# Output weights and gated products moved to another start address in larger tiles, in a three-stage attention and MoE kernel

## The chip, the cores and the metric

One core of one Trainium2 chip. The metric is the device time of one execution in microseconds (us), first instruction to last with what lies around them; less is better.

## What is computed

A linear attention with exponential features, then two gated feed-forward layers one after the other, all in float32:

```python
def _attn_ref(q, k, v, w_phi):            # 4 batches, 8 heads, 576 tokens, 64 per head
    ...
    num = einsum('bhsf,bhfd->bhsd', q_p, kv)
    den = einsum('bhsf,bhf->bhs', q_p, z)[..., None] + 1e-06
    return num / den
def _moe_ref(x, w_gate, w_val, w_out):    # x 2304 x 512, w_gate and w_val 512 x 1536, w_out 1536 x 512
    g = x @ w_gate
    return (silu(g) * (x @ w_val)) @ w_out
def _moe2_ref(x, w_gate, w_val, w_out):   # the same with sigmoid(g) in place of silu(g)
    ...
```

The output is `_moe2_ref(_moe_ref(attention))`, 2304 x 512.

## The kernel before

The first 150 us are attention. From there to the end TensorE runs the two layers, in four passes (`hh` 0 to 3; 0 and 1 are layer one, 2 and 3 layer two, each pass with half of the 1536 inner columns). A pass goes over five token blocks, four of 512 tokens and one of 256, and in each over three pairs of inner column groups (`p` 0 to 2). One `(hh, j, p)` is called a unit here; a layer has 24 units of a full block and 6 of the short block.

Every float32 operand is split into a high and a low part, and each product is made of three matmuls (high by high, high by low, low by high). A unit of a full block has

- seven products of a Strassen-like scheme (`product`, L1024), each twice, 84 matmuls of 256 columns. Their stationary operands are 128 x 128 pieces of the tiles `w0h`, `w0l` (and `w1`, `w2` for the other pairs), their moving operands are pieces of `xh`, `xl`;
- 24 matmuls of the output product of the unit before it (`accumulate`), put between the products in groups of 12, 9 and 3 by the tuple `ORDER`. In layer one (L1099) the output weights `o0h`, `o0l` are stationary and the gated products `uh`, `ul` move; in layer two (L1101) `uh`, `ul` are stationary and `o` moves, 512 columns each.

A unit of the short block has four products, 48 matmuls, and 12 accumulations of 512 columns (24 of 256 in layer one).

Between them ScalarE and VectorE bring products out of PSUM (`keep`, `add`), apply the gate, multiply (`gated`) and split the result into `uh`, `ul` (`gated_split`, `plan_halves`, L579 and L573). Output weights come to `o..l` by a DMA on SP's queue (`load_out`, L632) and are split in place by the same two engines; in the first slots they are made in place of being loaded (`split_home`). All DMAs of the kernel are issued on SP's queue; the order of all work is written out by hand in `TIMES`, one due time for each call.

Where operands lie in a partition follows from the tile sizes. The first 16384 bytes are scratch for DMA descriptors, then come four constants of 32 bytes each, so the pools `w0` and `w1` begin 128 bytes past a multiple of 256. All tiles of `w0`, `w1` and `w2` have sizes that are multiples of 512 bytes, and each matmul operand in them begins at a multiple of 512 bytes in its tile. So every `w` and `o` operand begins at 128 modulo 256 (`w2` on the right side too). The pool `stage` adds 192 bytes beyond multiples of 256 (two small tiles of 96), so every `x` and `u` operand begins at 64 modulo 256.

Of the kernel before, what the change touches and what calls it, by code (L numbers as in the profile page):

```python
# [11 lines left out]
R32 = mybir.dt.float32r  # L12
# [8 lines left out]
P = 128  # L21
# [3 lines left out]
DM = H * D  # L25
# [36 lines left out]
NQ = 256  # L62
# [14 lines left out]
ORDER = ((1, 2, "a", "b", 5, "c", "d", 4),  # L77
         (1, 5, "a", "b", 6, 3, 7, 2, "c", "d0", 4, "d1"))
ORDER_LAST = (1, 5, "a", 6, 3, "b", 7, 2, "c", 4, "d")


def as_float(bits):
# [349 lines left out]
class Plan:  # L432
# [10 lines left out]
    def at(self, t, fn, *args):  # L443
        if self.given:
            t = next(self.given[fn.__name__])
        self.events.append((t, len(self.events), fn, args))
# [7 lines left out]
def body(ctx: ExitStack, tc: tile.TileContext, qT, kT, v, w_phi2, wpk, out):  # L454
    nc = tc.nc
# [9 lines left out]
    pools = {w: ctx.enter_context(tc.tile_pool(name=w, bufs=1)) for w in ("w0", "w1")}  # L465
# [37 lines left out]
    def piece(name, dt=F32):  # L503
        return stage.tile([P, 1024], dt, tag="raw", name=name, bufs=RB)

    def scratch(name, dt=F32):
        return stage.tile([P, 768], dt, tag="tmp", name=name, bufs=TB)
# [62 lines left out]
    wts = {}  # L570

    def low(hi, lo, src):
        nc.vector.tensor_tensor(out=lo, in0=src, in1=hi, op=ALU.subtract)  # L573

    def plan_halves(t, views):

        def high():
            hi, _, src = views()
            nc.scalar.copy(hi, src)  # L579

        def rest():
            low(*views())

        at(t, high)
        at(t + 0.6, rest)

    def plan_slot(t, hh, p, gap=3.0, out=14.0):

        l, q = hh // 2, (hh % 2) * NPAIR + p
        a, s = {}, {}

        def home(i):
            w = i // 2
            if w not in a:
                a[w] = piece("a").rearrange("p (c q n) -> p c q n", c=2, q=4) if w < 2 else \
                    piece("a").rearrange("p (c n) -> p c n", c=2)
            return a[w][:, i % 2] if w == 2 else a[w][:, i % 2].rearrange("p q n -> p (q n)")  # L600

        def load(w):
            a[w] = piece("a").rearrange("p (c q n) -> p c q n", c=2, q=4)
            assert stored >= {("w", l, q, 2 * w), ("w", l, q, 2 * w + 1)}
            nc.sync.dma_start(out=a[w], in_=wf[l][q][:, w])

        begins = not isinstance(t, float)

        def sums(w):

            s[w] = scratch("s").rearrange("p (c q n) -> p c q n", c=2, q=3)
            a21, a11, a12, a22 = (a[w][:, :, k] for k in range(4))
            s1, s2, s4 = (s[w][:, :, k] for k in range(3))
            tt = (nc.gpsimd if begins else nc.vector).tensor_tensor
            tt(out=s1, in0=a21, in1=a22, op=ALU.add)
            tt(out=a21, in0=a11, in1=a21, op=ALU.subtract)
            tt(out=s2, in0=s1, in1=a11, op=ALU.subtract)
            tt(out=s4, in0=a12, in1=s2, op=ALU.subtract)

        def split(w, m):  # L620
            if (hh, p) not in wts:
                wts[hh, p] = [pools[f"w{p}"].tile([P, 2, 2, 7, P], R32, tag=f"w{p}{x}",
                                                  name=f"w{p}{x}{hh}") for x in "hl"]
            d, src = ((slice(0, 4), a), (slice(4, 7), s))[m]
            return *(x[:, w, :, d] for x in wts[hh, p]), src[w]

        def load_out():
            pool = pools[f"w{p}"]
            wts[hh, p, "o"] = [pool.tile([P, 2, DM], R32, tag=f"o{p}{x}", name=f"o{p}{x}{hh}")
                               for x in "hl"]  # L630
            assert stored >= {("w", l, q, 4), ("w", l, q, 5)}
            nc.sync.dma_start(out=wts[hh, p, "o"][1].bitcast(F32), in_=wfo[l][q])  # L632

        def split_out():
            hi, lo = wts[hh, p, "o"]
            return hi, lo, lo.bitcast(F32)

        def split_home():
            if (hh, p, "o") not in wts:
                wts[hh, p, "o"] = [pools[f"w{p}"].tile([P, 2, DM], R32, tag=f"o{p}{x}",  # L640
                                                       name=f"o{p}{x}{hh}") for x in "hl"]
            return *wts[hh, p, "o"], a[2]

        if not isinstance(t, float):
            for i, u in enumerate(t):
                e = plan_round(u, l, q, i, home)
                if i < 4 and i % 2:
                    at(e + 0.8, sums, i // 2)
                    for m in range(2):
                        plan_halves(e + 2.4 + 1.5 * m, partial(split, i // 2, m))  # L650
                elif i == 5:
                    plan_halves(e + 1.0, split_home)
            return

        for w in range(2):
            at(t + 2 * gap * w, load, w)
            at(t + 4.0 + 2 * gap * w, sums, w)
            for m in range(2):
                plan_halves(t + 6.0 + gap * (2 * w + m), partial(split, w, m))
        at(t + out, load_out)  # L660
        plan_halves(t + out + 4.0, split_out)

# [403 lines left out]
        v, o = places(r, j, 1, d)  # L1066
        nc.vector.tensor_tensor(out=o, in0=v, in1=places(r, j, 0, d)[1], op=ALU.mult)  # L1067

    def gated_split(r, j, f):
        n = BLOCKS[j][1]  # L1070
        v = r["c", f][:, 1].rearrange("p t n -> p (t n)")[:, :n]
        if ("u", f) not in r:
            r["u", f] = [pools["u"].tile([P, 2 * NQ], R32, tag=f"u{x}{f}", name=f"u{x}{f}")[:, :n]
                         for x in "hl"]
        return *r["u", f], v

    def part_of_group(m, s):
# [77 lines left out]
    def plan_out(t, r, hh, j, p, group):  # L1155

        n = BLOCKS[j][1]
        f, h = divmod("abcd".index(group[0]), 2)
        s = group[1:]
        at(t, accumulate, r, hh, j, p, f, h, s)  # L1160
        t += (3 if s else 6) * n / NQ * PT
        if s != "0" and p == NPAIR - 1 and f == 1 and not goes_on(hh + 1, j):
            if hh < 2:
                tiles = range(2) if h == 1 else ()
            else:
                tiles = (h,) if n == 2 * NQ else range(h)
            for i, k in enumerate(tiles):
                if hh % 2 == 1 and not goes_on(hh, j):
                    at(t - 8.0, out_load, hh, j, k)
                at(t + 0.1 + 1.2 * i, out_sum, hh, j, k)  # L1170
                at(t + OS + 1.5 * i, out_store, hh, j, k)
        return t

    def plan_unit(t, r, hh, j, p, last):


        full = BLOCKS[j][1] == 2 * NQ
        done = set()
        for k in ORDER_LAST if (hh, j, p) == (3, len(BLOCKS) - 1, NPAIR - 1) else ORDER[full]:
            if isinstance(k, str):  # L1180
                if last:
                    t = plan_out(t, *last, k)
                continue
            done.add(k)
            for w in range(2):
                at(t, product, r, hh, j, p, w, k)
                t += 6 * PT
            e = t + 0.1
            if full and k in (1, 5, 6):
                at(e, keep, r, k)  # L1190
            if full and k in (2, 3, 7):
                at(e, add, r, {2: 0, 3: 1, 7: 3}[k])
                e += 0.7
            for d in ([3] if full and k == 7 else [2] if k == 4 else
                      [0] if k in (2, 3) and done >= ({2, 3} if full else {2}) else []):
                at(e, gate, r, hh, j, d)
                at(e + 0.6, gated, r, j, d)
                if d != 3:
                    plan_halves(e + 1.2, partial(gated_split, r, j, d // 2))
        return t  # L1200

    def pool(name, side="left"):
# [23 lines left out]
    for hh in range(4):  # L1226
        begin.append(t)
        for i, j in enumerate(ROUTE[hh]):
            if hh % 2 == 1 and i < 2:
                xs[hh, j] = None  # L1230
            elif last:
                xprep.append((t, hh, j))
            for p in range(NPAIR):
                r = {}
                t = plan_unit(t, r, hh, j, p, last)
                free[hh, p] = t
                last = r, hh, j, p
# [13 lines left out]
    n = 6 * NPAIR  # L1251
    when = [R0A + (T0 - R0Z - R0A) * m / n for m in range(n)]
    for p in range(NPAIR - 1):
        plan_slot(when[6 * p:6 * p + 6], 0, p)
    for m in range(n - 6, n):
        plan_round(when[m], 0, NPAIR - 1, m % 6)
    plan_x_block(T0 - X00, 0, 0, XG)
    plan_slot(T0 - 3.0, 0, 2)
    for t, hh, j in xprep:
        plan_x_block(t - XL, hh, j, XG)  # L1260
    for hh in range(1, 4):
        plan_rounds(hh, begin[hh - 1] + RA, begin[hh] - RZ)
        for p in range(NPAIR):
            plan_slot(free[hh - 1, p] + SO, hh, p, SG)
# [43 lines left out]
```

## Time and profile before

| | us |
|---|---|
| median of 3 runs | 996.61 (989.23 to 996.86) |
| the profiled execution | 996.62 |
| its span, first instruction to last | 994.5 |
| TensorE matmul busy | 980.9 |
| VectorE busy | 692.4 |
| ScalarE busy | 527.2 |

All that the trace says is of the profiled execution. A matmul's busy time overlaps with that of the next, since matmuls are pipelined; what one costs in a stream is the time from its start to the start of the next, or a piece of the chain of work divided by its matmuls.

### The profile page before, as it was taken

Reading aid. Unit: us, or ns where it says so; the run is one execution under the profiler, and the core shown is the slowest. Engines: PE = TensorE matmul, PEld = TensorE weight load, DVE = VectorE, ACT = ScalarE, POOL = GpSimd, SP = SyncE. Lnnn points to the kernel's source line nnn. Section 1 sums busy time; section 2 is a strip of 40 time slices with the busy share of each in tenths; the row PEclk is TensorE's granted clock in tenths of the full one; section 3 lists DMA queues with packets and bytes.
Section 4 is the critical chain, followed back from the end, with each engine's and each line's share of the span. In section 5 each row is a group of like instructions: output and inputs, shape, how many; then the busy total and the mean of one; then the engine's idle time right before and its main releaser. Section 6 shows DMA issues by size and latency. Waiting matters only on the chain.

```text
span 994.5 us, 20911 instructions
## 1 busy us (share of the span) xinstructions
PE 980.9 (99%) x8632; PEld 891.5 (90%) x8632; DVE 692.4 (70%) x1220; ACT 527.2 (53%) x977; POOL 38.8 (4%) x40
## 2 busy tenths in 40 slices
PE   7999999999999999999999999999999999999998
PEld 6777778999999999999999999999999999999997
DVE  6999888938757795368787897486677834555343
ACT  5988977535545564264454574455546534334321
POOL 1433210000000000000000000000000000000000
PEclk9999999999999999999999999999999999999999
DMA  7566876436535532066554442446416002132011
GB/s 239 167 216 211 262 240 197 149 126 182 196 118 153 183 96 83 1 198 213 155 174 134 167 156 77 141 141 197 144 70 191 23 21 86 64 128 86 1 44 42
DMA packets 67551, 136.00 MB, mean 137 GB/s; under 512 B 9408, under 2 KB 35712, under 8 KB 67456
## 3 DMA queue, kind: packets, MB, share of 16 engines
q1 hardware_dynamic: 67456, 134.68, 42.4%
q8 instruction: 67, 1.10, 0.4%
q14 instruction: 28, 0.23, 0.1%
HBM read 94.66 MB, written 39.99 MB: 135 GB/s over the span
## 4 chain that ended last, share of the span: by engine, by line
PE 95%; DVE 3%; DMA 1%; ACT 0%; issue 0%; SPq 0%; DVEq 0%; ACTq 0%
PE a L1024 30%; PE b L1024 23%; PE c L1101 8%; PE c L1099 8%; PE d L1099 8%; PE d L1101 6%; PE d L787 5%; PE c L724 3%; PE w L688 3%; DVE sub L697 1%; DVE m L695 1%; PE w L751 1%; DMA xT<-nd 1%; DMA x<-kT 0%; ACT eq L771 0%
## 5 line engine op out<-in xcount | busy, mean ns | idle before, releaser
L1050 DVE TENSOR_TENSOR c<-b,c 128x512 f32<-128x512 f32 x96 | 66.0, 687 | 118.9 <-PE b L1024 109.9
L1062 ACT ACTIVATE c<-c 128x256 f32<-128x256 f32 x96 | 50.3, 525 | 147.0 <-DVE c L1050 147.0
L1044 ACT COPY c<-a 128x512 f32<-128x512 f32 x96 | 56.4, 587 | 111.9 <-PE a L1024 109.3
L573 DVE TENSOR_TENSOR ul<-c,uh 128x512 fp32r<-128x512 f32 (+1 forms) x120 | 75.8, 635 | 33.3 <-ACT uh L579 32.5
L579 ACT CAST uh<-c 128x512 fp32r<-128x512 f32 (+1 forms) x120 | 69.3, 580 | 41.6 <-DVE c L1067 33.3
L1024 PE MATMUL a<-xh,w0h 128*128 128x256 f32 x288 | 80.7, 280 | 0.0
L1024 PE MATMUL a<-xh,w1h 128*128 128x256 f32 x288 | 80.5, 280 | 0.0
L1024 PE MATMUL a<-xh,w2h 128*128 128x256 f32 x288 | 80.5, 279 | 0.0
L1024 PE MATMUL a<-xl,w0h 128*128 128x256 f32 x288 | 80.3, 279 | 0.0
L1024 PE MATMUL a<-xl,w2h 128*128 128x256 f32 x288 | 80.3, 279 | 0.0
L1024 PE MATMUL a<-xl,w1h 128*128 128x256 f32 x288 | 80.3, 279 | 0.0
L1024 PE MATMUL a<-xh,w0l 128*128 128x256 f32 x288 | 80.2, 279 | 0.0
L1024 PE MATMUL a<-xh,w2l 128*128 128x256 f32 x288 | 80.2, 279 | 0.0
L1024 PE MATMUL a<-xh,w1l 128*128 128x256 f32 x288 | 80.2, 278 | 0.0
L1067 DVE TENSOR_TENSOR c<-c 128x256 f32<-128x256 f32 (+1 forms) x96 | 52.9, 555 | 29.4 <-ACT c L1062 29.4
L1024 PE MATMUL b<-xh,w0h 128*128 128x256 f32 x224 | 62.5, 279 | 0.0
L1024 PE MATMUL b<-xh,w0l 128*128 128x256 f32 x224 | 62.4, 279 | 0.0
L1024 PE MATMUL b<-xh,w2l 128*128 128x256 f32 x224 | 62.4, 279 | 0.0
L1024 PE MATMUL b<-xh,w1l 128*128 128x256 f32 x224 | 62.4, 279 | 0.0
L1024 PE MATMUL b<-xl,w0h 128*128 128x256 f32 x224 | 62.4, 279 | 0.0
L1024 PE MATMUL b<-xh,w1h 128*128 128x256 f32 x224 | 62.4, 278 | 0.0
L1024 PE MATMUL b<-xl,w1h 128*128 128x256 f32 x224 | 62.4, 278 | 0.0
(183 smaller groups left out, 3028.5 us busy)
## 6 DMA issues: line engine op xcount, KB each, us to landing
raw<-wpk SPq DMA_DIRECT2D x72, 512.0 KB, 5.0
wf<-wcv SPq DMA_DIRECT2D x40, 256.0 KB, 2.8
a<-wf SPq DMA_DIRECT2D x20, 512.0 KB, 5.3
b<-xo SPq DMA_DIRECT2D x16, 512.0 KB, 6.1
part<-o SPq DMA_DIRECT2D x13, 512.0 KB, 6.2
o<-part SPq DMA_DIRECT2D x13, 512.0 KB, 4.7
wfo<-wcv SPq DMA_DIRECT2D x20, 256.0 KB, 4.9
v<-v SPq DMA_DIRECT2D x18, 264.0 KB, 7.3
```

Source lines behind the costliest of these rows:

```text
L573: nc.vector.tensor_tensor(out=lo, in0=src, in1=hi, op=ALU.subtract)
L579: nc.scalar.copy(hi, src)
L688: nc.tensor.matmul(r["ps"][:, i, n, c], r["x"][d, c, n * P:(n + 1) * P], w2[d], start=True, stop=True)
L724: nc.tensor.matmul(kv[qd, b][h // 2][u * 64:(u + 1) * 64, c * P:c * P + VW], e[r0:r1, h % 2, n, h // 2, s, u], r["v"][r0:r1, n, h], start= ...
L787: nc.tensor.matmul(pn[i * w:(i + 1) * w, :m], f, e[:, h, c, :m], start=(c == 0), stop=(c == 1))
L1024: nc.tensor.matmul(o, f[:, c], x[:, c], start=k == first and w == 0 and c == 0 and m == 0, stop=c == 1 and m == 2, skip_group_check=True)
L1044: nc.scalar.copy(part_of(r, d), parts(r, src))
L1050: nc.vector.tensor_tensor(out=c, in0=parts(r, "zy x"[d]), in1=c, op=ALU.add)
L1062: nc.scalar.activation(o, g, AF.Silu if hh < 2 else AF.Sigmoid)
L1067: nc.vector.tensor_tensor(out=o, in0=v, in1=places(r, j, 0, d)[1], op=ALU.mult)
L1099: nc.tensor.matmul(ps[:, :n], a[:, k], x, start=st, stop=sp)
L1101: nc.tensor.matmul(ps, x[:, k], a, start=st, stop=sp)
```

## The change

Each tile of output weights `o` and of gated products `u` becomes 128 elements (512 bytes) longer. The `o` operand begins 48 elements (192 bytes) into its tile, in both layers; the `u` operand stays at the start of its tile. 128 + 192 = 320, so `o` operands now begin at 64 modulo 256, as `x` and `u` do; `w` operands stay at 128. The DMA scratch shrinks from 16384 to 1024 bytes, by a multiple of 256, which makes room for the larger tiles. No instruction is added, removed or moved.

```diff
+U_AT = (0, 0)
+O_AT = (48, 48)
...
+        def out_tiles():
+            o = O_AT[l]
+            wts[hh, p, "o"] = [pools[f"w{p}"].tile([P, 2 * DM + P], R32, tag=f"o{p}{x}",
+                                                   name=f"o{p}{x}{hh}")[:, o:o + 2 * DM]
+                               .rearrange("p (c n) -> p c n", c=2) for x in "hl"]
+
         def load_out():
-            pool = pools[f"w{p}"]
-            wts[hh, p, "o"] = [pool.tile([P, 2, DM], R32, tag=f"o{p}{x}", name=f"o{p}{x}{hh}")
-                               for x in "hl"]
+            out_tiles()
...
         def split_home():
             if (hh, p, "o") not in wts:
-                wts[hh, p, "o"] = [pools[f"w{p}"].tile([P, 2, DM], R32, tag=f"o{p}{x}",
-                                                       name=f"o{p}{x}{hh}") for x in "hl"]
+                out_tiles()
             return *wts[hh, p, "o"], a[2]
...
-    def gated_split(r, j, f):
+    def gated_split(r, hh, j, f):
         n = BLOCKS[j][1]
         v = r["c", f][:, 1].rearrange("p t n -> p (t n)")[:, :n]
         if ("u", f) not in r:
-            r["u", f] = [pools["u"].tile([P, 2 * NQ], R32, tag=f"u{x}{f}", name=f"u{x}{f}")[:, :n]
-                         for x in "hl"]
+            o = U_AT[hh // 2]
+            r["u", f] = [pools["u"].tile([P, 2 * NQ + P], R32, tag=f"u{x}{f}", name=f"u{x}{f}")
+                         [:, o:o + n] for x in "hl"]
         return *r["u", f], v
...
-    nc = bacc.Bacc("TRN2", target_bir_lowering=False, num_devices=1)
+    nc = bacc.Bacc("TRN2", target_bir_lowering=False, num_devices=1, dynamic_dma_scratch_size=1024)
```

## Rows read from the trace of the kernel before

**Rows 1.** Page, busy time (share) x instructions of each engine.

```profile
PE 980.9 (99%) x8632; PEld 891.5 (90%) x8632; DVE 692.4 (70%) x1220; ACT 527.2 (53%) x977; POOL 38.8 (4%) x40
```

**Rows 2.** Page, chain that ended last: share of the span by engine.

```profile
PE 95%; DVE 3%; DMA 1%; ACT 0%; issue 0%; SPq 0%; DVEq 0%; ACTq 0%
```

**Rows 3.** Waits in total: who waited for whom, us, times, longest.

```profile
DVE c L1050 <- PE b L1024: 109.9, 34, 6.9
```

**Rows 4.** Stretches: length; PE, PEld, DVE, ACT, POOL busy; granted clock; DMA; GB/s.

```profile
200.00:300.00 100.00, 100.00 (x736) 94.69 (x735) 63.96 (x128) 48.54 (x101) 0.00 (x0) 1.00 0.50 159
...
700.00:800.00 100.00, 100.00 (x715) 93.38 (x714) 73.86 (x132) 55.12 (x96) 0.00 (x0) 1.00 0.30 98
```

**Rows 5.** Chain in order of time (start, us, what), layer one, full block.

```profile
212.90 1.42 PE a L1024 x12
214.31 1.41 PE b L1024 x12
215.73 1.39 PE c L1099 x6
...
226.27 1.37 PE a L1024 x12
...
228.33 1.42 PE a L1024 x12
```

**Rows 6.** Chain in order of time, layer two, full block.

```profile
618.53 1.39 PE a L1024 x12
619.91 1.36 PE b L1024 x12
621.27 1.37 PE c L1101 x6
622.65 1.37 PE d L1101 x6
...
633.62 1.39 PE a L1024 x12
```

**Rows 7.** Chain in order of time, layer one, short block.

```profile
259.23 1.41 PE a L1024 x12
...
267.71 1.41 PE a L1024 x12
```

**Rows 8.** Chain in order of time, layer two, short block.

```profile
678.91 1.39 PE a L1024 x12
...
687.15 1.39 PE a L1024 x12
```

**Rows 9.** Chain in order of time, before and after layer one's first accumulation.

```profile
156.04 1.36 PE a L1024 x12
...
172.17 1.42 PE a L1024 x12
```

**Rows 10.** Chain in order of time, where layer two's accumulations begin.

```profile
591.04 1.40 PE c L1101 x6
...
593.84 1.38 PE a L1024 x12
595.22 1.36 PE b L1024 x12
```

**Rows 11.** Instructions on PE in order of time, layer two: start, duration, line, names.

```profile
614.12 0.28 PE L1024 MATMUL b<-xh,w2l 128*128 128x256 f32 x1
614.23 0.39 PE L1101 MATMUL c<-o1h,uh 128*128 128x512 f32 x1
...
616.06 0.39 PE L1101 MATMUL d<-o1l,uh 128*128 128x512 f32 x1
616.29 0.28 PE L1024 MATMUL a<-xh,w2h 128*128 128x256 f32 x1
```

**Rows 12.** Instructions on tile o0l from 400 to 600 us: duration min/median/max, starts.

```profile
L579 ACT CAST o0h<-o0l x1: 1043/1043/1043, 562.8 to 562.8; 128x1024 fp32r<-128x1024 f32 x1
L573 DVE TENSOR_TENSOR o0l<-o0l,o0h x1: 1216/1216/1216, 574.0 to 574.0; 128x1024 fp32r<-128x1024 f32 x1
```

More of the change, by code (lines that the diff above doesn't have):

```diff
@@ L1198, in plan_unit @@
                 if d != 3:
-                    plan_halves(e + 1.2, partial(gated_split, r, j, d // 2))
+                    plan_halves(e + 1.2, partial(gated_split, r, hh, j, d // 2))
         return t
```

## The prediction

> **What bounds the kernel now.** I read the page first. TensorE is busy 99% of the span [rows 1] and holds 95% of the chain that ended last [rows 2]. The others wait for it: the largest wait of VectorE is 109.9 us for products [rows 3]. In the two layers no slice of TensorE is idle and the granted clock is 1.00, the higher level of 2.4 GHz, in both [rows 4]. So the only thing that a change of addresses can move is the pace of back-to-back matmuls, and that pace passes to the end almost whole.
>
> Next I read the chain in order of time, whose pieces give that pace. The same 12 products, same shapes, operands at the same places modulo 256 bytes, take 1.41 or 1.42 us in one place of layer one and 1.37 in another, 12 matmuls later in the same unit [rows 5]; in layer two they take 1.39 right after accumulations and 1.36 otherwise [rows 6]. That is 117.5 ns for a matmul at the one pace, called the 1.41 pace here, and 113.3 at the other, the 1.36 pace. A row of products mostly keeps the pace at which it begins. What sets it is the accumulations before it. Before layer one's first accumulation products run at 1.36; after it at 1.42 [rows 9]. Where layer two's accumulations begin, the first six still take 1.40, and the products after them 1.38 and then 1.36 [rows 10]; from there on each row of products is at the 1.36 pace after its first matmuls. So the two layers' accumulations leave TensorE at different paces, and they differ in one thing that an address can carry: what moves while what is loaded. In layer one `u` moves (64 modulo 256) while pieces of `o` are loaded (128); in layer two `o` moves (128) while `u` is loaded (64).
>
> The reader can see the whole price in two subtractions. A full unit, from its first product to that of the next, takes 228.33 - 212.90 = 15.43 us in layer one [rows 5] and 633.62 - 618.53 = 15.09 in layer two [rows 6], for the same 84 products and 24 accumulations of 512 columns. A short unit takes 8.48 [rows 7] and 8.24 [rows 8], for the same columns.
>
> **The change part by part.** *The scratch* shrinks by a multiple of 256, so it moves no operand modulo 256; all DMAs are on SP's queue and POOL issues none. Nothing is taken or added: 0.
>
> *The larger `u` tiles* keep `u` at 64: 0.
>
> *Writing and loading `o` at the new place.* A load, a cast and a subtraction for each of 12 slots. They are early: `o0h`'s cast runs at 562.8 for 1.04 us and the subtraction for `o0l` at 574.0 for 1.22 [rows 12], and layer two's first accumulation with them comes at 591.04 [rows 10]. Some 16 us cover them. Were both twice as long, nothing would move; without that cover they would cost the 2.3 us that they last, 27 us over 12 slots. I take 0.
>
> *Reading `o` at the new place* is all that is left. Now in both layers moving and loaded operand of an accumulation both begin at 64. At the edges: during the last product before a group, `x` (64) moves while `o` or `u` (64) is loaded; during the last accumulation of a group an operand at 64 moves while `w` (128) is loaded, in both layers.
>
> Two of these pairings stand in the trace at one matmul each. Equal places occur in layer two: the last product before a group has `x` moving and `u` loaded, both at 64, and the next matmul starts 0.11 us later, no stall [rows 11]. The last accumulation has `o` moving and `w` loaded, both at 128; the next starts 0.23 us later, and six of its kind take 1.37 [rows 6], so 0.228 each: no stall either [rows 11]. And after that matmul products settle at the 1.36 pace every time. Nothing shows a whole group at equal places; I bound it by the nearest rows: six accumulations between 1.36 (the columns of twelve products at the 1.36 pace) and 1.40 [rows 10]. I take 1.37, since the equal pairings that do occur cost no more than that.
>
> For the pace that the products get, the bounds are layer one's and layer two's. I take layer two's for both layers, because its groups end in an equal pairing and always leave the 1.36 pace. It is a choice: after the change a group's last matmul pairs 64 with 128, as layer one's does now.
>
> Sum: layer one at layer two's unit times. 24 full units x 0.34 us = 8.2; 6 short units x 0.24 = 1.4; together 9.6 us. The profiled execution took 996.62 (span 994.5 and 2.1 around it), within 0.01 of the median: 996.6 - 9.6 = 987.0.
>
> A rule speaks against any gain. The Trainium skill, page "SBUF — State Buffer", section "Who interferes with whom", gives TensorE two independent read ports, one for the moving operand and one for weight loads, and says that it never waits on anyone. By that rule start addresses are nothing and the sum is 0; the trace has 1.41 and 1.36 for equal products [rows 5, 6], which such ports alone don't explain, though it doesn't show that addresses are the cause either. The page "TensorE: Matmul & The Clock Gate", section "Back-to-back issue gap", gives a gap of N / 2.4 + 2.5 ns, 109.2 at 256 columns and 215.8 at 512; an estimate by it is 14.4 us for a full unit, which no row here reaches.
>
> **The rivals.**
>
> *Layer two falls to layer one's pace.* After the change both layers have the same places, so one pace may hold for both, and it may be 1.41: the group's last matmul (64 moving, 128 loaded) is the pairing that layer one has throughout. For it: in layer one that pairing leaves the 1.41 pace after groups of 12 and of 3 (1.42 and 1.41) [rows 5]. Against it: after the group of 9 it leaves the other (1.37) [rows 5]. It decides if rows of products in layer two start at 1.41 and stay. Then layer two takes layer one's unit times, 24 x 0.34 + 6 x 0.24 = 9.6 more: 1006.2. If the one row of 1.36 in each full unit goes as well, 0.05 x 48 = 2.4 more: 1008.6.
>
> *The paces alternate, or nothing changes.* In layer one the pace after a group alternates with the number of matmuls in it: 1.41 after 12, 1.36 after 9, 1.41 after 3. If the alternation stood the other way, six of the seven dozens of products in a unit would take 1.36: 5 x 0.05 x 24 = 6.0, and with the short units' 1.4 some 7 us less, 989.2. The lowest of the three times shown is 989.23, so the kernel before may already run in either order from one execution to the next. If the new places only reshuffle this, each layer lands between its bounds: 988 to 1001. If matmuls don't feel the places at all and the two layers' paces come from something else (their shapes, say), the time stays at 996.6. The Trainium skill's "SBUF — State Buffer", in the section named above, is on the side of this last one.
>
> *More than layer two's pace.* If equal places also removed the longer first matmuls of each row (1.39 against 1.36) and the accumulations' excess (1.37 against 1.36), a full unit would be 11 pieces of 1.36, 14.96, and a short one 6 pieces, 8.16: 0.13 x 48 + 0.08 x 12 = 7.2 under the sum, 979.8.
>
> *The gain doesn't reach the end.* TensorE 2% faster in layer one could come to wait for VectorE, busy 64% there [rows 4]. Layer two already runs at the faster pace with VectorE at 74% [rows 4]; I give it no chance of its own.
>
> **How the numbers follow.** The 1.36 pace in both layers: 0.46, between 980 and 990, likeliest 987.0. Unchanged or reshuffled: 0.29. The 1.41 pace in both: 0.25. A measurement of this kernel can tell about 1% from no change, here 10 us: under 986.6 and over 1006.6. Of the first case I put 0.28 below 986.6 and 0.18 above; the second lies within; of the third 0.17 lies above 1006.6 and 0.08 below. So faster 0.28, same 0.55, slower 0.17. The range 979 to 1006 takes in the best case and leaves out the third from its worked-out value up, 0.17 and a little under 979. The likeliest case's own range is 980 to 990.
>
> **What would show it.** Right: in the chain of the changed kernel, layer one's dozens of products at 1.36 (1.39 at a row's start) and six accumulations at 1.37; a full unit of 15.1 in both layers; layer two and attention unchanged to 0.5 us. First rival: 12 products at 1.41 in layer two and units of 15.4 there. Alternation: 1.36 and 1.41 side by side in both layers. No effect: the same rows as before, to 0.01. What would make the prediction wrong is above all the pace in which a group at equal places, closed by a 64-against-128 matmul, leaves the products: no row has that sequence. A group at equal places slower than 1.40 for six would be the second mistake.

## The result and the profile after

| | before | after |
|---|---|---|
| median, us | 994.94 (989.13 to 997.07, 12 runs) | 1000.93 (999.49 to 1002.41, 12 runs) |
| ratio of times | | 1.007, 95% interval 1.005 to 1.009 |
| the profiled execution, us | 996.62 | 1002.06 |
| its span, us | 994.5 | 1000.0 |

The change costs 0.7%. The interval leaves no doubt that the kernel is slower, though by less than the 1% that the prediction called no change. The time lies within the range of 979 to 1006, but 987.0 was forecast: the kernel went the other way.

The page of after, its span, the busy time of each engine, and the chain that ended last by engine:

```profile
span 1000.0 us, 20911 instructions
PE 986.1 (99%) x8632; PEld 897.6 (90%) x8632; DVE 693.6 (69%) x1220; ACT 528.1 (53%) x977; POOL 38.8 (4%) x40
PE 87%; DMA 1%; ACT 1%; DVE 1%; SPq 0%; issue 0%; ACTq 0%; DVEq 0%
```

The engines do the same work. As in [rows 1] TensorE is busy 99% of the span; the number of instructions is the same, and VectorE works 693.6 us where it worked 692.4. TensorE's share of the chain is 87% where it was 95% [rows 2]; what it lost lies in attention, since products and accumulations of the two layers hold the shares that they had, to 1%. The granted clock is 1.00 in every stretch of both layers, as before. So the question is the pace of matmuls, as it was before the change.

The chain of after in order of time (start, us, what), layer one, a full block, answering [rows 5]; `product` is at L1031 now, `accumulate` at L1107 in layer one and at L1109 in layer two:

```profile
214.98 1.36 PE a L1031 x12
216.34 1.36 PE b L1031 x12
217.70 1.38 PE c L1107 x6
219.08 1.36 PE d L1107 x6
220.44 1.42 PE a L1031 x12
...
226.10 1.39 PE c L1107 x6
227.48 0.68 PE d L1107 x3
228.16 1.42 PE a L1031 x12
229.58 0.70 PE d L1107 x3
230.28 1.36 PE a L1031 x12
```

The same view, layer two, answering [rows 6]:

```profile
603.42 1.36 PE a L1031 x12
...
608.88 1.41 PE a L1031 x12
...
616.60 1.41 PE a L1031 x12
618.02 0.70 PE d L1109 x3
618.72 1.36 PE a L1031 x12
```

Now the two layers are alike. After the group of 12 accumulations (`c` x6 and `d` x6) products run at the 1.41 pace, after the group of 9 (`c` x6 and `d` x3) as well, and after the group of 3 at the 1.36 pace. A dozen is the 12 matmuls of one product, and a unit has seven. A full unit takes 230.28 - 214.98 = 15.30 us in layer one (15.43 before) and 618.72 - 603.42 = 15.30 in layer two (15.09 before). Layer one had one dozen in seven at the 1.36 pace and now has two; layer two had all seven and now has two.

The balance of the two profiled executions, each matmul taken from its start to the start of the next and summed over a layer:

| us | before | after | difference |
|---|---|---|---|
| start to layer one's first accumulation | 169.1 | 171.4 | +2.3 |
| layer one, 2304 products | 270.4 | 269.1 | -1.3 |
| layer one, 576 accumulations of 512 columns | 134.4 | 132.9 | -1.5 |
| layer one, 144 accumulations of 256 columns | 17.0 | 17.2 | +0.2 |
| layer two, 2196 products | 251.0 | 256.2 | +5.2 |
| layer two, 647 accumulations | 148.6 | 149.1 | +0.5 |

Together +5.4, and the span grew by 5.5. The +2.3 ahead of the first accumulation is most likely scatter: attention has no operand at a new place, and in the profiled executions of before, after and of five of the kernels below, all five with the larger tiles and the smaller scratch, the first product starts at 149.8, 151.9, 150.2, 150.0, 150.1, 150.6 and 151.6. What the change did in these two executions is +5.7 in layer two, nearly all of it in products, whose own operands did not move, and -2.6 in layer one. The medians lie 6.0 apart; the executions of before spread over 8 us and those of after over 3, and the kernels below suggest that it is layer one's pace that spreads.

### The profile page after: what moved, and what is told of

Read it like the earlier page. It is cut to its first block, busy times and chain, and to the rows that moved or that the text cites. A ratio compares the mean times of both kernels' runs of the same rounds, so it can differ in the third digit from the quotient of the medians.

```text
span 1000.0 us, 20911 instructions
## 1 busy us (share of the span) xinstructions
PE 986.1 (99%) x8632; PEld 897.6 (90%) x8632; DVE 693.6 (69%) x1220; ACT 528.1 (53%) x977; POOL 38.8 (4%) x40
## 4 chain that ended last, share of the span: by engine, by line
PE 87%; DMA 1%; ACT 1%; DVE 1%; SPq 0%; issue 0%; ACTq 0%; DVEq 0%
PE a L1031 30%; PE b L1031 23%; PE c L1109 8%; PE c L1107 8%; PE d L1107 7%; PE d L1109 6%; PE d L794 2%; PE c L731 1%; PE w L695 1%; DMA den<-nd 1%; DMA xT<-nd 1%; PE w L758 0%; ACT ek L711 0%; ACT eq L778 0%; DVE o L1140 0%
## 5 line engine op out<-in xcount | busy, mean ns | idle before, releaser
L1069 ACT ACTIVATE c<-c 128x256 f32<-128x256 f32 x96 | 50.4, 526 | 150.1 <-DVE c L1057 150.1
L1031 PE MATMUL a<-xh,w0h 128*128 128x256 f32 x288 | 80.9, 281 | 0.0
L1031 PE MATMUL a<-xh,w1h 128*128 128x256 f32 x288 | 80.8, 281 | 0.0
L1031 PE MATMUL a<-xh,w1l 128*128 128x256 f32 x288 | 80.6, 280 | 0.0
L1031 PE MATMUL a<-xh,w0l 128*128 128x256 f32 x288 | 80.6, 280 | 0.0
L1031 PE MATMUL a<-xh,w2l 128*128 128x256 f32 x288 | 80.6, 280 | 0.0
L1031 PE MATMUL a<-xl,w0h 128*128 128x256 f32 x288 | 80.6, 280 | 0.0
L1031 PE MATMUL a<-xl,w1h 128*128 128x256 f32 x288 | 80.6, 280 | 0.0
L1031 PE MATMUL a<-xh,w2h 128*128 128x256 f32 x288 | 80.6, 280 | 0.0
L1031 PE MATMUL a<-xl,w2h 128*128 128x256 f32 x288 | 80.6, 280 | 0.0
L1031 PE MATMUL b<-xh,w1l 128*128 128x256 f32 x224 | 62.7, 280 | 0.0
L1031 PE MATMUL b<-xh,w0h 128*128 128x256 f32 x224 | 62.7, 280 | 0.0
L1031 PE MATMUL b<-xh,w2l 128*128 128x256 f32 x224 | 62.7, 280 | 0.0
L1031 PE MATMUL b<-xh,w1h 128*128 128x256 f32 x224 | 62.6, 280 | 0.0
L1031 PE MATMUL b<-xl,w1h 128*128 128x256 f32 x224 | 62.6, 280 | 0.0
L1031 PE MATMUL b<-xh,w2h 128*128 128x256 f32 x224 | 62.6, 280 | 0.0
L1031 PE MATMUL b<-xl,w2h 128*128 128x256 f32 x224 | 62.6, 280 | 0.0
```

The source lines that it names most:

```text
L1031: nc.tensor.matmul(o, f[:, c], x[:, c], start=k == first and w == 0 and c == 0 and m == 0, stop=c == 1 and m == 2, skip_group_check=True)
L1069: nc.scalar.activation(o, g, AF.Silu if hh < 2 else AF.Sigmoid)
```

## The experiments

All kernels but two (e12 and e16b, made from the kernel before) are the changed one with other values in its two tuples (elements of four bytes into the tile, layer one and layer two); three of them have one unused tile more. Where an operand begins modulo 256 is said as moving/loaded: in layer one's accumulations `u`/`o`, in layer two's `o`/`u`. Their difference is named the inside of a group: before, layer one had 64/128 (64 behind) and layer two 128/64 (64 past); after, both have 64/64 (equal). The end of a group is its last moving operand against `w` at 128: before, 64 behind in layer one and equal in layer two; after, 64 behind in both. The places of products are `x`/`w`, 64/128, except where the text says otherwise. The beginning of a group, where `x` moves while its first operand is loaded, has no column of its own below: with `x` and `w` fixed it follows from the inside and the end.

### Which part does it: scratch and tiles, layer one, layer two

**e1_tiles_only**, the larger tiles and the smaller scratch, all operands at their old places:

```diff
-O_AT = (48, 48)
+O_AT = (0, 0)
```

> The larger tiles and the smaller scratch stay, the output weights go back to the start of their tiles (128 modulo 256 in both layers). If the places of the output weights alone made the change: full units of 15.43 us in layer one and 15.09 in layer two as before, and a time equal to that of before, 989 to 997. If the tiles' size, the scratch or the new layout of memory behind it did it (the attention part is 2 us longer in the changed kernel): about 1000, with the units of before and a longer attention.

994.77 us (10 runs; before 996.46 beside it), ratio 0.9998 (0.997 to 1.0026). Its rows are those of before: six accumulations in 1.39 or 1.40 in layer one, 1.41 after 12 and 3, 1.36 after 9. Scratch and sizes cost nothing; the places do it.

**e2_layer1_only** and **e3_layer2_only**, the new place in one layer alone:

```diff
-O_AT = (48, 48)
+O_AT = (48, 0)     # e2; e3 has (0, 48)
```

> Output weights at 64 modulo 256 in layer one alone. If places set the pace: layer one's full units at 15.30 as in the changed kernel, layer two's at 15.09 as before; some 3 us under the slower executions of before, 991 to 994. If the pace has another cause: no difference between the layers, 1000.

> Output weights at 64 modulo 256 in layer two alone. If places set the pace: layer two's full units go from 15.09 to 15.30, layer one's stay at 15.2 to 15.43; 24 x 0.21 = 5 us more than before, 994 to 1002. If not: as before.

e2: 994.53, ratio 0.999 (0.9971 to 1.0009). e3: 1002.63, ratio 1.0058 (1.0032 to 1.0084). By the balance made as above, layer one and layer two take 419.4 and 399.7 us in e2, 421.7 and 405.3 in e3, against 421.8 and 399.6 before and 419.2 and 405.3 after. So the layers don't touch each other: each takes the time that goes with its own places, and the loss is layer two's.

The spread goes with layer one's places too. With those of before it is 8.8 us (before, 31 runs), 7.7 (e1) and 10.7 (e3); with those of after it is 2.9 (after) and 2.9 (e2).

### Two paces to set apart: that of accumulations and that of products

**e4_u_moved_l1** gives layer one 192/128, 64 past inside as layer two had before, with 64 past at the end too. **e5_layer1_as_layer2** gives it 128/64, layer two's own numbers inside and at the end:

```diff
-U_AT = (0, 0)
-O_AT = (48, 48)
+U_AT = (32, 0)     # e4; e5 has (16, 0)
+O_AT = (0, 0)      # e4; e5 has (48, 0)
```

> Output weights at 128 as before; in layer one alone the gated products begin 128 bytes into their tiles, at 192 modulo 256, so that the moving operand of an accumulation begins 64 bytes past the one that is loaded, as it does in layer two before. If that distance sets the pace: layer one's full units at 15.09, short ones at 8.24, 987 or a little less. If the place counts only where both are equal, or not at all: 15.43 and the time of before.

> In layer one alone gated products begin at 128 and output weights at 64 modulo 256: every pairing of a moving and a loaded operand is then that of layer two before, at both ends of a group too. If the pairing at the end of a group sets the pace of the products after it (moving and loaded equal there): layer one's full units at 15.09 us and short ones at 8.24, 9.6 us under the slower executions of before, 987, and little spread between executions. If layer one has another reason for its pace (stationary and moving swapped, the order of work): dozens of products at 1.41 in layer one, 994 to 998.

e4: 997.24, ratio 1.0016 (0.9997 to 1.0036); far from the 987 expected. Its chain, layer one:

```profile
217.16 1.39 PE c L1107 x6
218.55 1.37 PE d L1107 x6
219.93 1.41 PE a L1031 x12
```

The second six accumulations have come down to 1.37, as in layer two [rows 6], but the products stay at 1.41 after every group. So these are two things: the pace inside a group, and the pace in which it leaves the products.

e5: 989.39 (9 runs, 987.66 to 990.21; before 996.07), ratio 0.9931 (0.9911 to 0.9952). It is faster than before, by 0.7% and clear of noise, and faster than after in every run. Its chain, layer one:

```profile
213.31 1.39 PE a L1031 x12
214.70 1.36 PE b L1031 x12
216.06 1.37 PE c L1107 x6
217.43 1.37 PE d L1107 x6
218.81 1.39 PE a L1031 x12
...
226.33 1.39 PE a L1031 x12
...
228.41 1.39 PE a L1031 x12
```

A unit of 228.41 - 213.31 = 15.10, the rows of layer two [rows 6] to 0.01. Layer one takes 413.4 us, 8.4 less than before. So layer one's slower pace came from its places: with layer two's places it takes layer two's pace, whatever its gate and whichever of `u` and `o` moves. (For one other pair of places the layers do differ, in e17 below.)

### Is it the pairing at the end of a group?

e4 and e5 differ in the last accumulation (192 or 128 moving while `w` at 128 is loaded), and layer two, too, went from an equal end to one of 64 behind. If an equal end alone gave the 1.36 pace, any inside would do. Three kernels with other ends were made, then three more:

```diff
-U_AT = (0, 0)
-O_AT = (48, 48)
+U_AT = (16, 0)     # e6; e7 (16, 0), e8 (32, 32), e13 (48, 48), e14 (48, 48), e15 (48, 32)
+O_AT = (0, 16)     # e6; e7 (32, 32), e8 (32, 0), e13 (48, 32), e14 (0, 48), e15 (16, 48)
```

> Places modulo 256. Layer one: gated products 128, output weights 128, so equal inside a group and equal at its end (moving 128, product weights 128), 64 against 128 at its beginning. Layer two: output weights 192, gated products 64, so the moving operand is 128 past the loaded one inside a group, 64 past it at the end, equal at the beginning. If the pairing at a group's end decides: products of layer one at 1.36 for a dozen, of layer two at 1.41. If the pairing inside decides: layer one as in the changed kernel (1.41 after groups of 9 and 12, 1.36 after 3). If the one at the beginning decides: layer two at 1.36.

> Places modulo 256. Layer one: gated products 128, output weights 0, so equal at a group's end, 128 past inside, 64 past at the beginning. Layer two: output weights 0, gated products 64, so at a group's end the moving operand is at 0 and the loaded one at 128, equal at the beginning. If the end decides: layer one's dozens of products at 1.36, layer two's at 1.41. If equality inside or at the beginning is needed: layer one at 1.41.

> Places modulo 256. Layer one: gated products 192, output weights 0, so at a group's end the moving operand is 64 past the loaded one, as at its beginning. Layer two: output weights 128, gated products 192, so equal at a group's end, 64 behind inside as in layer one before, 128 apart at the beginning. If the end decides: layer one's dozens at 1.41, layer two's at 1.36. If the pairing inside decides: layer two takes layer one's pace of before, 1.41 after groups of 12 and 3, 1.36 after 9.

> Places modulo 256. Layer one: gated products 0, output weights 64: at a group's end the moving operand (0) is 128 from the loaded one (128), equal at the beginning, 64 behind inside; layer two of e7 in layer one. Layer two: both at 0: 128 apart at the end, 64 past at the beginning, equal inside. If ends 128 apart leave products at 1.36 whatever lies inside: dozens of 1.36 in both layers, six accumulations at 1.36 in layer two (226.7 ns each, as between equal places in e6), units of 15.0, about 988. If the inside decides: layer two's products at 1.41 as in layer one of e6, 1000.

> Places modulo 256. Layer one: gated products 0, output weights 128: 128 apart at the end and inside, 64 behind at the beginning. Layer two: output weights 64, gated products 0: 64 behind at the end, 64 past at the beginning and inside. If the end decides: 1.36 in layer one, 1.41 (or a mixture as in the changed kernel) in layer two. If the inside decides: layer two at 1.36 as before, layer one mixed.

> Places modulo 256. Layer one: gated products 0, output weights 192: 128 apart at the end and at the beginning, 64 past inside. Layer two: output weights 64, gated products 192: 64 behind at the end, 128 apart at the beginning and inside. If the end decides: 1.36 in layer one, 1.41 or mixed in layer two. If the inside decides: layer one at 1.36 too (64 past), layer two mixed, so this kernel tells nothing on layer one and is read with e14.

One run each: e6 999.75, e7 996.27, e8 998.1, e13 998.85, e14 990.02, e15 1000.63. For each layer, worked out over all its groups from the start of one matmul to that of the next: the pace at which dozens run behind groups of 12, 9 and 3, and the means of accumulations of 512 columns and of products in ns, with the few matmuls left out that began late. Each row is one execution.

| inside | end | where | after 12, 9, 3 | accumulation | product |
|---|---|---|---|---|---|
| equal | 64 behind | both layers after | 1.41, 1.41, 1.36 | 229.7, 229.9 | 116.8, 116.6 |
| equal | equal | e6, layer one | 1.41, 1.41, 1.41 | 226.9 | 117.2 |
| equal | 128 away | e13, layer two | 1.41, 1.41, 1.41 | 228.7 | 118.1 |
| 64 past | equal | layer two before | 1.36, 1.36, 1.36 | 229.1 | 114.3 |
| 64 past | equal | e5, layer one | 1.36, 1.36, 1.36 | 229.3 | 114.6 |
| 64 past | 64 behind | e14, layer two | 1.36, 1.36, 1.36 | 229.1 | 113.8 |
| 64 past | 64 past | e4, layer one | 1.41, 1.41, 1.41 | 230.9 | 117.7 |
| 64 past | 128 away | e15, layer one | 1.41, 1.41, 1.41 | 231.2 | 117.7 |
| 128 away | 64 past | e6, layer two | 1.41, 1.41, 1.36 | 231.7 | 116.3 |
| 128 away | equal | e7, layer one | 1.41, 1.36, 1.36 | 231.7 | 116.1 |
| 128 away | 64 behind | e15, layer two | 1.36, 1.41, 1.41 | 232.4 | 115.4 |
| 128 away | 128 away | e14, layer one | 1.36, 1.41, 1.36 | 233.3 | 114.1 |
| 64 behind | 64 behind | layer one before | 1.41, 1.36, 1.41 | 232.6 | 117.3 |
| 64 behind | 128 away | e13, layer one | 1.36, 1.36, 1.36 | 232.0 | 114.3 |
| 64 behind | 128 away | e7, layer two | 1.36, 1.36, 1.36 | 231.9 | 113.8 |
| 64 behind | 64 past | e8, layer one | 1.41, 1.36, 1.41 or 1.36, 1.41, 1.36, half the units each | 232.5 | 115.4 |
| 64 behind | equal | e8, layer two | 1.41 or 1.36 for a whole unit, in turn | 232.6 | 115.9 |

Each pattern stands behind at least 88% of the groups of its size (23 of 26 at the least), mostly behind all of them; e8 has two.

Layer one of e6 in the chain, equal inside and at the end:

```profile
216.09 1.36 PE c L1107 x6
217.45 1.36 PE d L1107 x6
218.81 1.41 PE a L1031 x12
```

Six accumulations in 1.36, the shortest of all, and the products behind them at 1.41. So an equal end is not enough for the 1.36 pace, and a 64-behind end does not prevent it (layer two of e14). Neither is the inside alone enough: 64 past stands with all dozens at 1.36 and with all at 1.41. The accumulations' own means do go with the inside: 226.9 to 229.9 ns at equal places, 229.1 to 231.2 at 64 past, 231.7 to 233.3 at 128 away and 231.9 to 232.6 at 64 behind. The ranges touch, and layer two's rose from 229.1 to 229.9 when its places became equal.

Layer two of e8 shows what the table's patterns can't: that the pace in which a group is entered counts. Its chain, the first dozen behind a group of 3 and behind a group of 12, in two units that follow each other:

```profile
599.33 1.38 PE a L1031 x12
...
604.86 1.41 PE a L1031 x12
...
614.72 1.41 PE a L1031 x12
...
620.35 1.38 PE a L1031 x12
```

Here a group of 12 turns the pace (12 times from 1.36 to 1.41, 12 times back) and groups of 9 and 3 keep it, so whole units run at the one pace and at the other in turn. In layer one of e8 it is the group of 12 that keeps the pace (13 times 1.41, 11 times 1.36, and once, behind a late operand, not), and those of 9 and 3 turn, 11 times each way. In after a group leaves its own pace, however it is entered: groups of 12 leave 1.41, entered 43 times at 1.36 and 6 times at 1.41, and groups of 3 leave 1.36, entered 44 times at 1.41 and twice at 1.36. In the rows in which every group is entered at one pace only, the two kinds can't be told apart.

### The products' own places

**e9_x_192**, **e10_x_128**, **e11_x_0** move `x` against `w` and keep the accumulations at e5's 128/64 in both layers. An unused tile ahead of the pool moves `x`, and the tuples make up for it:

```diff
-U_AT = (0, 0)
-O_AT = (48, 48)
+U_AT = (48, 32)    # e9; e10 (0, 48), e11 (32, 16)
+O_AT = (48, 0)
...
+    ctx.enter_context(tc.tile_pool(name="gap", bufs=1)).tile([P, 32], F32, name="gap")   # e9; 16 in e10, 48 in e11
```

> All accumulations at the places of layer two before (moving operand 128, loaded 64), and the products' own moving operand, x, at 192 in place of 64, 64 past their weights (128) in place of 64 behind. If the products' own distance sets their pace: one pace after every group; the 256-column accumulations that stood 64 ahead took 118.1 ns, so dozens of 1.41 to 1.42, some 17 us over the kernel with the same accumulations and x at 64 (989), 1005. If the group before them sets it: 1.36 after the same settling, 989.

> The same with x at 128, equal to the product weights. If the products' own distance sets their pace: the 256-column accumulations at equal places took 119.7 ns, so dozens of 1.44, 4608 x 5.4 ns = 25 us over 989, about 1013. If the group before sets it: 989.

> The same with x at 0, 128 from the product weights. If the products' own distance sets their pace: the 256-column accumulations 128 apart took 118.4 ns, so dozens of 1.42, about 1008. If the group before sets it: 989.

One run each: e9 1005.29, e10 1012.66, e11 1010.88. Layer one of e10, where `x` and `w` both begin at 128:

```profile
214.90 1.44 PE b L1032 x12
216.34 1.38 PE c L1108 x6
```

All dozens take 1.44, the accumulations still 1.37 to 1.38; a unit is 15.57. In e9 (192/128) dozens take 1.41 or 1.42 everywhere, a unit 15.42, in e11 (0/128) 1.42 to 1.44, 15.52. So equal places, with the lowest means for accumulations, are the worst for products. Only with `x` 64 behind `w`, where the kernel before has it, did any dozen take 1.36; there it has two paces, elsewhere none better than 1.41.

### The same places, another count or another start

**e12_before_again** is the kernel before, once more under a profile, since its times lie between 989 and 998:

> The kernel before once more, unchanged, for its spread (989 to 999 over some 40 executions, two clusters). If layer one's alternation stands one way or the other from execution to execution: in an execution near 990 layer one's full units take 15.2 us with 1.36 in all but a few dozens, in one near 997 they take 15.43; attention differs by up to 2 us between executions of any of these kernels.

997.43 us, units of 15.43 and 15.09: the pattern of [rows 5] again. The execution beside it took 991.61; no profile caught the kernel before near 990. One thing differs from the first profile. Its chain ahead of layer one's first accumulation, where [rows 9] have 1.36:

```profile
156.79 1.41 PE a L1024 x12
```

So products that no accumulation of a layer precedes have both paces too, in two executions of one kernel. Of the 16 profiles with `x` at its old place, 13 have 1.41 there and 3 have 1.36.

**e16b_even_groups** is the kernel before with some accumulations of layer one, in both of its passes, due later, so that in two units of three the groups are 12, 6 and 6 in place of 12, 9 and 3:

```diff
+            if fn.__name__ == "accumulate" and args[1] < 2 and args[3] < 2 and args[-1] == "0":
+                t += 205
```

> The kernel before with three accumulations of layer one moved behind the last product of the unit, in two of three units: their groups are 12, 6 and 6 in place of 12, 9 and 3. Same work, same places. If an odd number of accumulations turns the pace and an even one keeps it: in those units no dozen changes pace, the one before the last six takes 1.41 where it took 1.36 (if layer one stands at 1.41 otherwise); in the third units, with 9 and 3, it takes 1.36 as before. 0.05 x 16 = 0.8 us more. If something other than the number turns it: 1.36 in all units.

993.72 us, one run. In the chain, a unit with even groups, and then one with a group of 9:

```profile
194.38 1.40 PE c L1101 x6
195.78 1.36 PE a L1026 x12
197.14 1.40 PE d L1101 x6
198.54 1.36 PE a L1026 x12
...
208.14 1.36 PE b L1026 x12
209.50 1.39 PE c L1101 x6
210.90 0.70 PE d L1101 x3
211.59 1.42 PE a L1026 x12
213.01 0.69 PE d L1101 x3
213.70 1.37 PE a L1026 x12
```

The places are those of before, 64 behind inside, and the accumulations at 1.40 show it. Here the odd groups turn the pace, 9 to 1.41 and 3 back, and the even ones keep it, as was expected if the number counts and as in [rows 5]; of layer one's groups of 512 columns all 12 of 9 and 3 turn it, and 55 of the 56 of 12 and 6 that had no wait keep it. (It is no rule for other places: in layer two of e8 groups of 12 and 6 turn.) But it is 1.36 that they keep here, where before keeps 1.41. The 1.36 came in near 180 us, where TensorE waited for VectorE between a group of six and the products behind it (0.83 us idle): products ran at 1.41 and more up to there, and at 1.36 behind it. In the later half of layer one, behind the group of 12 that begins at 361.75, the 1.41 order is back, with no wait at that point; what turned it there is not seen.

**e17_inside_64_past** has 64 past inside in both layers, with a 64-behind end:

```diff
-U_AT = (0, 0)
-O_AT = (48, 48)
+U_AT = (0, 48)
+O_AT = (32, 48)
```

> Both layers in the setting of e14's layer two: moving operand at 64, loaded one at 0, so 64 past inside a group and at its beginning, 64 behind at its end. Layer one: gated products 64, output weights 0; layer two: output weights 64, gated products 0. If the three distances are all that counts: full units of 15.05 us in both layers, 24 x 0.38 + 24 x 0.04 = 10 us less than the executions of the kernel before near 997, plus 1 to 2 for the short blocks: 985 to 987, with little spread. If swapping stationary and moving matters beyond the distances: layer one at 15.2 to 15.4, 989 to 995.

988.26 us (12 runs; before 996.64), ratio 0.9951 (0.9918 to 0.9984): it is faster than both kernels too. Eight of its runs lie between 986.6 and 988.6, one at 993.5 and three between 997.8 and 999.8, so the small spread that was expected is not there. Its profile, of a run of 988.08, shows how. TensorE's instructions in order of time (start, duration, line, names), where layer one's second pass begins:

```profile
359.96 0.39 PE L1107 MATMUL c<-uh,o2h 128*128 128x512 f32 x1
360.61 0.51 PE L1107 MATMUL c<-ul,o2h 128*128 128x512 f32 x1 [0.26 <-DVE ul L577]
```

and the chain before it, behind it, and 100 us on:

```profile
336.86 1.36 PE b L1031 x12
...
363.42 1.41 PE a L1031 x12
...
460.66 1.42 PE a L1031 x12
...
466.32 1.36 PE a L1031 x12
```

Up to 360 us layer one's dozens are at 1.36 in every full unit. Then the second matmul of a group starts 0.65 us after the first, and from there every dozen is at 1.41, with the same places, order and counts, until the short block's 256-column accumulations begin near 466 us. The accumulations go with it, from a mean of 229.1 ns ahead of the late one to 233.6 behind it. So the places don't fix the pace: the same stream has both, and the one lasted here for some 40 dozens. Layer two, with the same places, has 1.36 nearly throughout.

A late operand is not enough to turn the pace, nor is it needed. All profiles but that of e16b have this matmul late, by 0.43 to 0.65 us from start to start. In e8 the order turns there, in e7 and e15 for the four dozens behind it; in before, after and e5 it stays. The instructions of e5 and then its chain behind them:

```profile
361.77 0.39 PE L1107 MATMUL c<-uh,o2h 128*128 128x512 f32 x1
362.37 0.50 PE L1107 MATMUL c<-ul,o2h 128*128 128x512 f32 x1 [0.20 <-DVE ul L577]
```

```profile
365.17 1.38 PE a L1031 x12
366.54 1.36 PE b L1031 x12
```

In e16b the order is turned back with no wait. A delay put in on purpose was not tried. What the profiles do show is which kernels get over a turn: in layer one of e5 the groups of 12 and 3 that were entered at 1.41, four in all, left 1.36 again, while in e17 nearly all groups keep the pace in which they are entered, 1.36 or 1.41. That fits the times, 2.6 us from lowest to highest in e5 and 13.2 in e17.

## Why the prediction was wrong, point by point

**What bounds the kernel** was right. In the two layers only TensorE's pace has moved, and it passed to the end whole: +5.4 in the balance, +5.5 in the span.

**Scratch, larger tiles, writing and loading `o`**: each costed at 0. Scratch and tiles are 0 (e1, 0.9998 with 0.997 to 1.0026). Writing and loading `o` at its new place has no run of its own; the balance, 5.4 of 5.5 us, leaves next to nothing for it.

**Places bear on the paces** was right, and is now shown: e5 differs from after in two tuples and is 11.5 us shorter (989.39 against 1000.93), and e10 is 23 us longer than e5 by the place of `x`. The Trainium skill's page "SBUF — State Buffer", section "Who interferes with whom", gives TensorE two independent read ports and says that it never waits on anyone; read as covering start addresses too, as the prediction's rival did, it would give all these kernels the same time, and the runs do not agree.

**"What sets it is the accumulations before it"** was too much. It rests on [rows 9], 1.36 ahead of layer one's first accumulation and 1.42 behind it, and that 1.36 was luck: the same kernel has 1.41 there in e12. (The dozen at 1.37 in [rows 5] is the seventh of its unit, 13.4 us behind the first, and not 12 matmuls later.)

**Reading `o` at equal places, 1.37 for six** was right in size: 1.36 to 1.39 after, 1.5 us saved in layer one's 576 accumulations and 0.5 lost in layer two's. Bounds of 1.36 to 1.40 held it.

**The step that failed** is the one called a choice: "I take layer two's for both layers, because its groups end in an equal pairing and always leave the 1.36 pace." Three things were wrong in it. The equal end that it gives as its reason is one that the change takes away, as its next sentence says: after, a group ends 64 behind in both layers. The pace after a group was read as a property of the group's end; e6 (equal end, 1.41 after each group) and e14 (64-behind end, 1.36 after each in layer two) show that the end does not settle it. And it was taken to hold where the inside changes, though the only group that "always" left 1.36 was 64 past inside. After the change the groups leave 1.41, 1.41 and 1.36. The term forecast at 24 x 0.34 + 6 x 0.24 = 9.6 us of gain came out as 2.6 of gain in layer one and 5.7 of loss in layer two.

**The rivals.** The one that came true by its sign is "the paces alternate": 1.36 and 1.41 side by side in both layers. By its mechanism it did not: in after it is not the number's being odd that turns the pace, since groups of 12 turn 1.36 to 1.41 and groups of 9 leave 1.41 as it is. Its 988 to 1001, in which 1000.9 is the far end, is not worked out: the bounds of both layers give 987.0 to 1006.2. So that the time lies in the stated range is owed to the rivals' width, not to the mechanism. Its remark that the kernel before may run in either order from one execution to the next has support: e16b runs the same places with 1.36 as the pace that is kept in the first pass, e8 has both orders in one execution, and layer one of e14 is the alternation that stands the other way, 1.36, 1.41, 1.36, in a kernel of 990.02; its layer one is 6.9 us shorter than before's (414.9 against 421.8). That before's executions near 990 run in that order was not seen in a profile. The first rival (1.41 throughout, 1006.2) was too dark by the two dozens in seven that stay at 1.36. "More than layer two's pace" is not reached by any kernel; e17's 986.6 is the lowest time.

**What would show it** named the right rows: dozens at 1.41 in layer two and side by side with 1.36 is what told the alternation apart at first sight, and "a group at equal places, closed by a 64-against-128 matmul: no row has that sequence" was the open point that decided. With no row for it, the 0.46 on the forecast had only the equal end to rest on.

**What stays open**: what decides which of the two paces a group leaves. Neither the inside's difference, nor the end's, nor the number of matmuls settles it alone, and the same sequence has both (e17, e8). The table suggests that inside and end both bear on it, e16b that the number does, and the counts in e8, e16b and e17 that the pace ahead of the group does at some places; the pace turned at a wait in e8, e16b and e17, and at a like one in e5 it did not. Rows of one execution can hide a second order, so those of the kernels with one run are weak by themselves; after, e4 and e5 have nine or more runs each that lie within 3 us. A rule that would have forecast after's 1.41, 1.41, 1.36 was not found, and why places bear on the pace at all is open too.

## What to carry to other kernels

Where TensorE is the bound and matmuls stand back to back, the start addresses of moving and loaded operands can be worth up to 2%, as here, and the places with the lowest time for one kind of matmul (equal, for these accumulations) can be the worst for another. To set places, copy a whole pattern that a trace shows running well, inside, end and order, as e5 did; don't put a new one together from pieces that were seen in other sequences. Then run it several times: e17's layer one copied e14's layer two and ran at 987 to 989 in 8 of 12 executions only. And when a kernel's times fall into two clusters, read the pace of equal pieces in the chain before judging a change of a few us, and don't take the order in one profile for the kernel's only one.

## What the runs showed of the hardware

- Equal matmuls run at paces that differ with where their operands begin modulo 256 bytes. 256 columns, start to start: 113.3 or 117.8 ns with moving 64 behind loaded, 117.8 at 64 past (e9), 119.9 at equal places (e10), a mean of 119.0 at 128 away (e11). 512 columns, means of a layer in the table above: 226.9 to 229.9 at equal places, 229.1 to 231.2 at 64 past, 231.7 to 233.3 at 128 away or 64 behind. Equal places have the lowest mean for the one kind (e6) and the highest for the other (e10). The Trainium skill's page "TensorE: Matmul & The Clock Gate", section "Back-to-back issue gap", has N / 2.4 + 2.5 ns for a matmul by itself, which the prediction's 14.4 us took for a stream; an estimate by it is 109.2 and 215.8; the shortest here are 113.3, and six accumulations in 1.36 us, 226.7 each (e6).
- Products with `x` 64 behind `w` have two paces, 4% apart, and a row of them mostly keeps the one in which it begins. In e17 a dozen took 1.36 us ahead of an accumulation that was late by some 0.4 us (0.65 from start to start in place of 0.23), and 1.41 in the 40 dozens behind it; in e5 an accumulation as late (0.60) changed nothing.
- At some places the pace that a group of accumulations leaves is that in which it was entered, kept or turned (both layers of e8, layer one of e16b and e17); at others it is the group's own (after). Kernels whose layer one stands at before's places or e17's spread over 7.7 to 13.2 us from execution to execution, those with after's, e4's or e5's over 2.5 to 2.9.
- A kernel can be shortened by start addresses alone: e5 saves 6.7 us (0.9931) by moving two operands by 64 and 192 bytes in one of two layers.
